# Clearing the last sums behind the last value product, leftover mixer groups behind the last projections, late weight loads deferred

## The chip, the cores and the metric

The kernel runs on one core of a Trainium2 chip. Its time is the device time of one launch in microseconds (us); where several runs are made, their median stands for the kernel. A core has five engines with queues of their own: TensorE (PE, matrix products; its weight loads are shown as PEld), VectorE (DVE), ScalarE (ACT), GpSimd (POOL) and SyncE (SP), which here only issues transfers (DMA) between HBM and the on-chip memory SBUF. Matrix products write to PSUM, an accumulator memory of eight banks per partition; a bank holds 512 columns in f32.

## The reference

Two layers are computed one after the other with the same weights. Each is an attention block and then a mixer over the tokens, both with a residual sum (S = 2048 tokens, D = 640, 32 heads of 20, F = 1536):

```python
def _A_ref(x, wqkv, wo):
    qkv = (x @ wqkv).reshape(B, S, 3, H, Dh).transpose(2, 0, 3, 1, 4)
    q, k, v = qkv[0], qkv[1], qkv[2]
    scores = jnp.einsum("bhqd,bhkd->bhqk", q, k) * (Dh ** -0.5)
    p = _softmax(scores, axis=-1)
    o = jnp.einsum("bhqk,bhkd->bhqd", p, v)
    return o.transpose(0, 2, 1, 3).reshape(B, S, D) @ wo

def _B_ref(x, w1, b1, w2, b2):
    h = _layernorm(x, axis=-1)
    u = _gelu(jnp.einsum("bsd,sf->bdf", h, w1) + b1)
    y = jnp.einsum("bdf,fs->bds", u, w2) + b2
    return y.transpose(0, 2, 1)

x = A_x
x = x + _A_ref(_layernorm(x, axis=-1), A_wqkv, A_wo)
x = x + _B_ref(_layernorm(x, axis=-1), B_w1, B_b1, B_w2, B_b2)
x = x + _A_ref(_layernorm(x, axis=-1), A_wqkv, A_wo)
x = x + _B_ref(_layernorm(x, axis=-1), B_w1, B_b1, B_w2, B_b2)
```

The weights and x are bf16; sums and the residual are kept in f32.

## The kernel before

**Tiling.** The 2048 tokens are 16 tiles of 128 and 4 blocks of 512. The 32 heads are 8 groups of 4; a group's heads lie in the four quarters of 32 partitions, so that four products of 32 rows run side by side. A unit of attention is one group, one block of queries and one tile of keys: four products of 128 keys by 512 queries, called cells. Cells are collected into tiles of three and two PSUM banks in turn (`S`, pools `s3` and `s2`), and ACT turns each tile into exponentials with one instruction (L710). Some cells go to the bank `Dt` instead, and DVE and POOL compute their exponentials with shifts and polynomials (L539 to L599). The products with the values (L1252, `emit_PV`) sum in the bank `acc`. At the end of a block DVE transposes, divides by the sum of exponentials and transposes back (`finish_run`, L747 to L771); the result is `attnT`.

**Planner.** `attention` writes the order of PE, DVE, ACT and POOL by hand: while the program is built it keeps a clock for each engine (`pem["t"]`, `dvm["t"]`, `acm["t"]`) from fixed costs, and puts whatever fits into the gaps beside the exponentials. These fillers (`add_fill`, `fill_step`) are projections of keys, queries and values, transposes, output projections, and the mixer's first product. Each filler group sums in a bank (`misc` or `Dt`), and its evacuation is a `Proc` of rank 1 that `submit` hands to the clocks of DVE or ACT. Outside of attention `submit` puts the evacuation into the program at once (`force`). Where a gap stays empty, products with zero weights (`zero_wave`, L699) keep PE busy. `landing[tt]` is the time at which the planner expects tile tt of x.

**The start of layer 0** (`TokenFeed.begin`, from L1425). SP loads x tiles 0 to 3, the first halves of the key and query weights (`w_raw`, through `load_raw` and `load_w`, L1431) and of the value weights (into `x1last`), then x tiles 4 and 5, the second halves of the three weights, and then x tiles 6 to 15 (L1439), each as soon as the tile six places ahead is normalized: its buffer is one of six. DVE takes the statistics (L823, L826), POOL the root (L840), DVE normalizes (L844), PE transposes (L1151), and the fillers for values (L1127), keys and queries (L1103) follow. ACT copies the first four groups of key and query weights into their padded form (L1474), DVE the second four (L1476).

**The end of an attention.** The mixer's first product is summed over the tokens in parts. The last part but one (L994, 6 matmuls of 128 x 320 per group, two groups per row tile of F) is among the fillers, and each group is added to a row held in SBUF (L1002). What is left of them when the last exponential has been issued is emitted behind the last value products, with banks from `tail_alloc`: `Dt`, `misc` and the third bank of `sums[0]` in turn. Then `end_tiles` handles the last two token tiles: it clears the two `S` tiles (`sums`) with four zero waves of 512 columns, ACT copies the residual into them (L893) and loads the table for GELU (L894), PE adds the projection of the last pair of head groups (L898), and DVE, ACT and POOL normalize twice over (L908 to L926): statistics of each tile, ACT's copy back to SBUF (L909), ACT's normalized first tile (L923), DVE's second (L926). Meanwhile PE runs `WARM_WAVES` = 14 zero waves of four matmuls.

**The mixer.** `mixer_head` multiplies the last two tiles with w1 (L1665), adds the row (L1668), takes GELU (L1671) and starts the second product with w2 (L1687; whole tiles in L1678). In layer 0 it feeds the start of layer 1 (`MixFeed`); in layer 1 it runs through all 16 tiles and writes the output (L1737, L1742). The weights w2 are loaded in eight parts of 768 KB (L1700), the residual in tiles of 320 KB (`x1in`, L1553 and L1718). `after_vector(inst)` makes an instruction wait for the last DVE instruction that is already in the program.

Of the kernel before, what the change touches and what calls it, by code (L numbers as in the profile page):

```python
# [23 lines left out]
D = 640  # L24
# [22 lines left out]
HALF = 0.14  # L47
# [19 lines left out]
WARM_WAVES = 14  # L67
# [10 lines left out]
def kernel(  # L78
# [12 lines left out]
    nc = tc.nc  # L91
# [128 lines left out]
    def attention(st, x_in_ap, x_mid, uacc_l, feed, feed_stack):  # L220
# [65 lines left out]
        class Proc:  # L286
# [17 lines left out]
            def step(self):  # L304
# [8 lines left out]
                if not self.steps:  # L313
                    self.eng["procs"].remove(self)
                    if self.after is not None:
                        self.after(end)

        def submit(proc):
            proc.eng["procs"].append(proc)
            if not in_attention[0]:  # L320
                force(proc)
# [562 lines left out]

        def end_tiles(sums):
            assert check_hT_dead() and TAIL == 2
            gp = NG // 2 - 1
            attnT = attnT_tiles[LASTQB + 1][gp]
            for t in sums:
                for c in (0, 512):  # L890
                    zero_wave(t[:, c:c + 512], True, True)
            for t, x1 in zip(sums, x1_end):
                nc.scalar.copy(out=t[:, 0:D], in_=x1)  # L893
            nc.scalar.activation(out=warm_act[:, 0:1], in_=mhalf[:, 0:1], func=ACT.Gelu_apprx_tanh, scale=1.0)  # L894
            for ttl, t in enumerate(sums):
                for odd in range(2):
                    for c0, c1 in Y_CUTS:
                        pe(nc.tensor.matmul(t[:, c0:c1], lhsT=attnT[:, 256 * odd + ttl * 128:256 * odd + (ttl + 1) * 128],  # L898
                                            rhs=wo_pad[:, 2 * gp + odd, c0:c1], start=False, stop=(odd == 1),
                                            skip_group_check=True))  # L900
            halves = [[t[:, 0:D // 2], t[:, D // 2:D]] for t in sums]
            st = [stat.tile([128, 2, nc.vector.BN_STATS_DIM], F32, name="bnst") for _ in range(2)]
# [8 lines left out]
            def spread(i):  # L911
# [12 lines left out]
                                 scale=rs[0][:, 0:1])  # L924
            spread(1)
            nc.vector.tensor_scalar(out=h2_view[:, NT - 1, :], in0=x1_end[1], scalar1=mv[1][:, 0:1], scalar2=rs[1][:, 0:1],  # L926
                                    op0=ALU.subtract, op1=ALU.mult)

        def add_fill(key, prio, mms, evac, w, ready=0.0, allow=None, after=None, wave=None, cells=None, cost=None,
# [446 lines left out]
        sums = [s_tile(w)[:].rearrange("p a b -> p (a b)") for w in (3, 2)]  # L1376
        tail_banks = deque([Dbank.alloc, misc.alloc, lambda: sums[0][:, 1024:1536]])

        def tail_alloc():
            tail_banks.rotate(-1)  # L1380
            return tail_banks[-1]()
        while fs["cur"] is not None or fill_queue:
            fill_step(tail_alloc)
        assert not dvm["procs"] and not acm["procs"]
        end_tiles(sums)
        idle = pp["acc"].tile([128, 512], F32, name="acc")
        for _ in range(WARM_WAVES):
            zero_wave(idle, True, True)
        p1.close()

    class TokenFeed:
# [33 lines left out]
        def begin(self, cx):  # L1425
# [4 lines left out]
            def load_w(dst, coff):  # L1430
                nc.sync.dma_start(out=dst, in_=A_wqkv[:, coff:coff + D // 2].rearrange("(dt p) n -> p dt n", p=128))  # L1431

# [12 lines left out]
            for tt in range(4, 6):  # L1445
                load_x(tt)
            load_raw(0, 1)
            load_raw(1, 1)
            load_w(self.wv[:, 1], 2 * D + D // 2)
            landing = {tt: 3.2 + 0.5 * tt for tt in range(4)}  # L1450
# [38 lines left out]
            def start_tile(tt):  # L1489
# [5 lines left out]
                def after(e):  # L1495
                    if tt + 6 < NT:
                        load_x(tt + 6)
                        landing[tt + 6] = max(14.0 + 0.5 * (tt - 2), e + 3.0)
                        start_tile(tt + 6)
                    cx.t_fill(tt, h[tt], e + DVE_TO_PE, lambda: out_h.discard(tt))  # L1500
                cx.ln_proc(xin[tt][:], False, dst, 2.5 + 0.01 * tt, landing[tt], after,
# [293 lines left out]
```

## Time and profile before

| | us |
|---|---|
| median of 3 runs | 1771.04 (1770.96 to 1772.27) |
| the profiled execution | 1772.69 |
| its span | 1770.9 |
| PE busy | 1683.8 (95%) |
| ACT busy | 1676.4 (95%) |
| DVE busy | 1538.4 (87%) |
| POOL busy | 386.6 (22%) |
| first and last exponential of layer 0 | 17.72 and 825.52 |
| first and last exponential of layer 1 | 866.50 and 1699.73 |

The granted clock of TensorE is 0.999 of full speed over the execution. The profile shows one execution; its time is that of the launch, and its span is from the first to the last instruction on the core. Lines such as L710 are lines of the kernel before. A matmul's shown end is modelled, and successive instructions of one engine overlap by a part of a microsecond, so that the time from one start to the next is shorter than the shown length. "Idle before" is the time in which an engine stood still ahead of an instruction, with what ended it.

### The profile page before, as it was taken

To read this page: it belongs to the slowest core of one execution; us is meant where nothing else is said; L and a number is where in the kernel's file an instruction comes from. 1 tells how busy PE (TensorE), PEld (TensorE's weight loads), DVE (VectorE), ACT (ScalarE), POOL (GpSimd) and SP (SyncE) were. 2 spreads that over 40 slices of the span, in tenths; PEclk is the share of its full clock that TensorE was granted. 3 is DMA by queue.
4 is the path that set the end of the run, shared out by engine and by line. 5 is a ranking of instruction groups with operands and counts; after the bars stand their busy time and mean duration, and the time that the engine had idled before them with its cause. 6 is when DMAs were issued, how large, how long until landed. Compare 5 with 4: busy or idle time off the path is not lost. (4 is left out here: it accounts for less than half of the span.)

```text
span 1770.9 us, 42935 instructions
## 1 busy us (share of the span) xinstructions
PE 1683.8 (95%) x17978; PEld 671.5 (38%) x18058; DVE 1538.4 (87%) x2361; ACT 1676.4 (95%) x1509; POOL 386.6 (22%) x599
## 2 busy tenths in 40 slices
PE   8999999999999999999999999999999999999999
PEld 3333333333333344444444433233333333444445
DVE  7479999999999999998543369999999999999972
ACT  8999999999999999998779999999999999999970
POOL 2112222232233223221000011122223232322200
PEclk9999999999999999999999999999999999999999
DMA  3200000010112110123322110000001220101345
GB/s 116 37 4 1 1 2 2 12 35 2 35 52 81 38 36 14 39 75 118 111 81 73 40 35 1 1 2 31 31 1 61 68 80 13 61 3 54 103 120 178
DMA packets 103010, 81.85 MB, mean 46 GB/s; under 512 B 50976, under 2 KB 87456, under 8 KB 102816
## 3 DMA queue, kind: packets, MB, share of 16 engines
q1 hardware_dynamic: 97280, 71.22, 13.4%
q0 software_dynamic: 5536, 7.88, 1.4%
q8 instruction: 141, 2.31, 0.6%
q14 instruction: 53, 0.43, 0.1%
HBM read 55.48 MB, written 23.59 MB: 45 GB/s over the span
## 5 line engine op out<-in xcount | busy, mean ns | idle before, releaser
L710 ACT ACTIVATE P<-S 128x1536 bf16<-128x1536 f32 (+2 forms) x1441 | 1629.0, 1368 | 15.6 <-PE S L640 15.3
L640 PE MATMUL S<-QTq,KT 32*128 32x512 bf16 (+1 forms) x4484 | 580.2, 337 | 68.9 <-ACT P L710 49.6
L599 POOL TENSOR_SCALAR ey<-ew 128x512 f16<-128x512 uint16 x496 | 306.7, 618 | 1017.2 <-DVE et L573 387.3
L640 PEld LDWEIGHTS <-KT 32*128 32x128 bf16 x5134 | 234.3, 91 | 537.9 <-issue 509.4
L1252 PE MATMUL acc<-P,Vaug 128*32 128x512 bf16 (+1 forms) x4470 | 361.5, 344 | 0.8 <-ACT P L710 0.3
L539 DVE TENSOR_SCALAR ew<-Dt 128x512 int32<-128x512 f32 x498 | 339.4, 681 | 18.7 <-PE Dt L640 12.4
L699 PE MATMUL acc<-zr,zw 128*32 128x512 bf16 x4436 | 344.0, 383 | 1.4 <-POOL zr L151 1.2
L582 DVE SCALAR_TENSOR_TENSOR Pd<-ew,et 128x1024 int16<-128x1024 int16 x249 | 310.7, 1248 | 1.5
L573 DVE SCALAR_TENSOR_TENSOR et<-ey,ew 128x1024 f32<-128x1024 f16 x249 | 303.5, 1219 | 2.0
L640 PE MATMUL Dt<-QTq,KT 32*128 32x512 bf16 (+1 forms) x650 | 191.5, 332 | 0.0
L569 DVE TENSOR_TENSOR ey<-ey 128x1024 f16<-128x1024 f16 x249 | 172.6, 693 | 0.5
L1252 PEld LDWEIGHTS <-Vaug 128*32 128x32 bf16 x5120 | 101.5, 94 | 169.1 <-issue 159.4
L699 PEld LDWEIGHTS <-zw 128*32 128x32 bf16 x4636 | 116.2, 96 | 100.6 <-issue 53.7
L840 POOL TENSOR_TENSOR rstd<-veps,mhalf 128x1 f32<-128x1 f32 x60 | 54.3, 906 | 252.8 <-DVE veps L838 206.5
L1252 PE MATMUL acc<-Pd,Vaug 128*32 128x512 bf16 (+1 forms) x650 | 97.5, 334 | 0.7 <-issue 0.5
L1103 PE MATMUL misc<-hh,wq_pad 128*128 128x512 bf16 x277 | 82.6, 383 | 2.1 <-issue 1.6
L994 PEld LDWEIGHTS <-w1st 128*128 128x128 bf16 x672 | 52.6, 97 | 57.6 <-issue 44.7
L747 DVE STREAM_TRANSPOSE T<-acc 128x512 f32<-128x512 f32 (+1 forms) x81 | 56.3, 695 | 20.4 <-PE acc L1252 20.0
L1043 PE MATMUL misc<-wo_pad,attnT 128*128 128x320 bf16 x384 | 73.5, 302 | 0.3 <-DVE x1s L1055 0.2
L994 PE MATMUL misc<-x1last,w1st 128*128 128x320 bf16 x384 | 71.6, 302 | 0.0
L1103 PE MATMUL misc<-hh,wk_pad 128*128 128x512 bf16 x211 | 64.8, 383 | 2.0 <-issue 1.3
L359 DVE CAST KT<-misc 128x512 bf16<-128x512 f32 x48 | 32.8, 683 | 19.8 <-PE misc L1103 19.7
(145 smaller groups left out, 1085.9 us busy)
## 6 DMA issues: line engine op xcount, KB each, us to landing
w2s<-in_B_w_dram SPq DMA_DIRECT2D x16, 768.0 KB
uacc<-ustg POOLq DMA_DIRECT2D x24, 320.0 KB, 2.7
x1in<-xd SPq DMA_DIRECT2D x24, 320.0 KB
w1st<-in_B_w_dram SPq DMA_DIRECT2D x24, 256.0 KB
xd<-x2s SPq DMA_DIRECT2D x16, 320.0 KB
xin<-xd SPq DMA_DIRECT2D x16, 320.0 KB
w1st<-in_B_w_dram SPq DMA_DIRECT2D x24, 192.0 KB
xd<-x1s SPq DMA_DIRECT2D x12, 320.0 KB
```

The lines of the kernel that those rows point to most:

```text
L539: nc.vector.tensor_scalar(out=w[:, slot, :], in0=Dt[:, :], scalar1=127.0 * FIX, scalar2=0.0, op0=ALU.add, op1=ALU.max)
L569: nc.vector.tensor_tensor(out=y, in0=y, in1=y, op=ALU.mult)
L573: nc.vector.scalar_tensor_tensor(out=box["t"][:, 0:512 * k], in0=ve_y.pop(p)[:, 0:512 * k], scalar=MANT_C * MANT_K ** 2, in1=frac, op0=ALU ...
L582: nc.vector.scalar_tensor_tensor(out=bits, in0=whole, scalar=128.0, in1=box["t"][:, 0:512 * k], op0=ALU.mult, op1=ALU.add)
L599: return engine.tensor_scalar(out=out_ap, in0=in_ap, scalar1=MANT_K / FIX, scalar2=-MANT_K * MANT_S, op0=ALU.mult, op1=ALU.add)
L640: pe(nc.tensor.matmul(out_ap[:, c0:c0 + w], lhsT=KT[32 * j:32 * j + 32, g, kt * 128:(kt + 1) * 128], rhs=get_QT(st, qb)[32 * j:32 * j + 32 ...
L699: pe(nc.tensor.matmul(bank[32 * j:32 * j + 32, 0:w], lhsT=zw[:], rhs=zr[:, :, 0:64].to_broadcast([128, w // 64, 64]), start=start, stop=st ...
L710: nc.scalar.activation(out=P[:, 0:ncs, :].rearrange("p a b -> p (a b)"), in_=St[:, 0:ncs, :].rearrange("p a b -> p (a b)"), func=ACT.Exp, ...
L994: pe(nc.tensor.matmul(t[:, 0:w], lhsT=w1_of[(p, ft)][:, sti, :], rhs=rows_in[sti][:, c0:c1], start=(sti == 0), stop=(sti == n_in - 1)))
L1043: pe(nc.tensor.matmul(t[:, 0:w], lhsT=attnT[g][:, ttl * 128:(ttl + 1) * 128], rhs=wo_pad[:, g, c0:c1], start=(g == 0), stop=(g == NG - 1)))
L1103: pe(nc.tensor.matmul(t[:, :], lhsT=wpad[:, dt_, g, :], rhs=hT[:, dt_, tb * 512:(tb + 1) * 512], start=(dt_ == 0), stop=(dt_ == NDT - 1)))
L1252: pe(nc.tensor.matmul(acc[32 * j:32 * j + 32, a0:a0 + w], lhsT=Vaug[:, (kt * H + hh_) * VW:(kt * H + hh_) * VW + 32], rhs=P[:, slot, c0:c0 ...
```

## The change

It has three parts.

In `TokenFeed.begin` the second halves of the key, query and value weights are no longer loaded behind x tiles 4 and 5. `load_rest` issues them when tile 5 has been normalized, and each of these loads waits for the DVE instruction that is then the last one in the program (`after_vector`). The planner's expected landing of x tile tt + 6 becomes 16.5 + 0.5 tt instead of 14.0 + 0.5 (tt - 2).

Behind the last value product the two sums are cleared at once, each with a wave of 512 columns and one of 128 instead of two of 512. Then leftover fillers are emitted for 1.3 us of the planner's clock, and a group that is begun is finished.

In `end_tiles`, fillers that are then still left come behind the last projections. Their evacuations are held (`held`) and put into the program later: one while POOL computes the second root, the others behind the last normalized tile. The number of warming waves falls by four for each such group, and not below four.

```diff
--- before.py
+++ after.py
@@ -315,8 +315,13 @@
                     if self.after is not None:
                         self.after(end)
 
+        held = []
+
         def submit(proc):
             proc.eng["procs"].append(proc)
+            if not in_attention[0] and proc.rank == 1 and held:
+                held.append(proc)
+                return
             if not in_attention[0]:
                 force(proc)
 
@@ -882,13 +887,12 @@
             ln_open.append(tt)
             ln_proc(x1s[:], True, dst, 3, end + DVE_NEXT, after)
 
-        def end_tiles(sums):
+        rest_fills = [0]
+
+        def end_tiles(sums, alloc):
             assert check_hT_dead() and TAIL == 2
             gp = NG // 2 - 1
             attnT = attnT_tiles[LASTQB + 1][gp]
-            for t in sums:
-                for c in (0, 512):
-                    zero_wave(t[:, c:c + 512], True, True)
             for t, x1 in zip(sums, x1_end):
                 nc.scalar.copy(out=t[:, 0:D], in_=x1)
             nc.scalar.activation(out=warm_act[:, 0:1], in_=mhalf[:, 0:1], func=ACT.Gelu_apprx_tanh, scale=1.0)
@@ -898,6 +902,16 @@
                         pe(nc.tensor.matmul(t[:, c0:c1], lhsT=attnT[:, 256 * odd + ttl * 128:256 * odd + (ttl + 1) * 128],
                                             rhs=wo_pad[:, 2 * gp + odd, c0:c1], start=False, stop=(odd == 1),
                                             skip_group_check=True))
+            held.append(None)
+            while fs["cur"] is not None or fill_queue:
+                fill_step(alloc)
+            rest_fills[0] = len(held) - 1
+            held.pop(0)
+
+            def emptied(n):
+                while n and held:
+                    force(held.pop(0))
+                    n -= 1
             halves = [[t[:, 0:D // 2], t[:, D // 2:D]] for t in sums]
             st = [stat.tile([128, 2, nc.vector.BN_STATS_DIM], F32, name="bnst") for _ in range(2)]
             mv = [stat.tile([128, nc.vector.BN_AGGR_DIM], F32, name="mv") for _ in range(2)]
@@ -923,8 +937,10 @@
             nc.scalar.activation(out=h2_view[:, NT - 2, :], in_=x1_end[0], func=ACT.Identity, bias=shift[:, 0:1],
                                  scale=rs[0][:, 0:1])
             spread(1)
+            emptied(1)
             nc.vector.tensor_scalar(out=h2_view[:, NT - 1, :], in0=x1_end[1], scalar1=mv[1][:, 0:1], scalar2=rs[1][:, 0:1],
                                     op0=ALU.subtract, op1=ALU.mult)
+            emptied(len(held))
 
         def add_fill(key, prio, mms, evac, w, ready=0.0, allow=None, after=None, wave=None, cells=None, cost=None,
                      act=None, gate=None, fed=False):
@@ -1374,17 +1390,21 @@
             emit_PV(n)
 
         sums = [s_tile(w)[:].rearrange("p a b -> p (a b)") for w in (3, 2)]
-        tail_banks = deque([Dbank.alloc, misc.alloc, lambda: sums[0][:, 1024:1536]])
+        for t in sums:
+            zero_wave(t[:, 0:512], True, True)
+            zero_wave(t[:, 512:D], True, True, HALF / 2, D - 512)
+        tail_banks = [sums[0][:, 1024:1536], None, None]
 
         def tail_alloc():
-            tail_banks.rotate(-1)
-            return tail_banks[-1]()
-        while fs["cur"] is not None or fill_queue:
+            bank = tail_banks.pop()
+            return bank if bank is not None else Dbank.alloc() if len(tail_banks) == 1 else misc.alloc()
+        room = pem["t"] + 1.3
+        while fs["cur"] is not None or (fill_queue and pem["t"] < room):
             fill_step(tail_alloc)
+        end_tiles(sums, tail_alloc)
         assert not dvm["procs"] and not acm["procs"]
-        end_tiles(sums)
         idle = pp["acc"].tile([128, 512], F32, name="acc")
-        for _ in range(WARM_WAVES):
+        for _ in range(max(4, WARM_WAVES - 4 * rest_fills[0])):
             zero_wave(idle, True, True)
         p1.close()
 
@@ -1428,7 +1448,9 @@
             raw, xin = {}, {}
 
             def load_w(dst, coff):
-                nc.sync.dma_start(out=dst, in_=A_wqkv[:, coff:coff + D // 2].rearrange("(dt p) n -> p dt n", p=128))
+                inst = nc.sync.dma_start(out=dst, in_=A_wqkv[:, coff:coff + D // 2].rearrange("(dt p) n -> p dt n", p=128))
+                if (0, 1) in raw:
+                    after_vector(inst)
 
             def load_raw(i, part):
                 raw[(i, part)] = self.wp.tile([128, NDT, D // 2], BF16, name="w_raw")
@@ -1444,9 +1466,11 @@
             load_w(self.wv[:, 0], 2 * D)
             for tt in range(4, 6):
                 load_x(tt)
-            load_raw(0, 1)
-            load_raw(1, 1)
-            load_w(self.wv[:, 1], 2 * D + D // 2)
+
+            def load_rest():
+                load_raw(0, 1)
+                load_raw(1, 1)
+                load_w(self.wv[:, 1], 2 * D + D // 2)
             landing = {tt: 3.2 + 0.5 * tt for tt in range(4)}
             landing.update({4: 9.5, 5: 10.0})
             wpads = (wk_pad, wq_pad)
@@ -1495,8 +1519,10 @@
                 def after(e):
                     if tt + 6 < NT:
                         load_x(tt + 6)
-                        landing[tt + 6] = max(14.0 + 0.5 * (tt - 2), e + 3.0)
+                        landing[tt + 6] = max(16.5 + 0.5 * tt, e + 3.0)
                         start_tile(tt + 6)
+                    if tt == 5:
+                        load_rest()
                     cx.t_fill(tt, h[tt], e + DVE_TO_PE, lambda: out_h.discard(tt))
                 cx.ln_proc(xin[tt][:], False, dst, 2.5 + 0.01 * tt, landing[tt], after,
                            allow_apply=lambda: len(out_h) < 4, cheap=0.04)
```

## The prediction

> **What bounds the kernel now.** I read the stretches of both attentions first, then ScalarE's (ACT's) timeline, then the start and the two ends of attention in order of time, and last the chain that ended last.
>
> In the timeline of ACT alone (start, length, line, kind, count, in brackets the idle time before and what ended it), layer 0's exponentials are two unbroken rows:
>
> ```profile
> 17.72 495.66 ACT L710 ACTIVATE P<-S 128x1536 bf16<-128x1536 f32 x438 [3.14 <-PE S L640]
> 513.53 311.99 ACT L710 ACTIVATE P<-S 128x1536 bf16<-128x1536 f32 x276 [0.16 <-PE acc L1252]
> ```
>
> From 17.72 to 825.52 ACT stands still for 0.16 us, so layer 0 lasts as long as its 714 exponentials. Only three things count there: when the first one starts, how many there are, and what follows the last.
>
> The groups of ACT by shape, in the window of 17 to 826 us, give the mix:
>
> ```profile
> L710 ACT ACTIVATE P<-S 128x1536 bf16<-128x1536 f32 x357 | 564.6, 1582 | 3.5 <-PE S L640 3.1 <-PE acc L1252 0.2
> L710 ACT ACTIVATE P<-S 128x1024 bf16<-128x1024 f32 x356 | 413.9, 1163 | 0.0
> ```
>
> Neighbours overlap, so the means are no steps. The means differ by 0.42 us for 512 columns. Together with one tile of 512, 714 tiles in 807.6 us give a step s of a 1024 tile: 714 s + 357 x 0.42 - 0.42 = 807.6, so s = 0.92 us.
>
> The timeline of the start shows why the first exponential is at 17.72:
>
> ```profile
> 9.19 28.23 SPq L1439 DMA_DIRECT2D x0in<-in_A_x_dram  x10
> 14.12 0.68 DVE L359 CAST KT<-Dt 128x512 bf16<-128x512 f32 x1
> 14.85 0.84 PE L1127 MATMUL Dt<-x1last,hh 128*128 128x320 bf16 x5 [0.46 <-DVE KT L359]
> 16.15 0.49 DVE L823 BATCH_NORM_STATS2 bnst<-x0in 128x6 f32<-128x320 bf16 x1 [1.35 <-DMA x0in<-in_A_x_dram]
> 16.56 0.67 DVE L361 TENSOR_SCALAR QTq<-misc 128x512 bf16<-128x512 f32 x1
> 17.29 0.59 PE L640 MATMUL S<-QTq,KT 32*128 32x512 bf16 x5 [1.59 <-DVE QTq L361]
> ```
>
> VectorE (DVE) waits 1.35 us for tile 6 of x, whose load SP issues at 9.19, behind the three late weight loads. The copy of the first Q stands behind those statistics, and scores and exponentials behind it.
>
> The timeline of layer 0's end:
>
> ```profile
> 825.96 0.85 PE L994 MATMUL misc<-hh,w1st 128*128 128x320 bf16 x5
> 827.18 0.45 DVE L771 STREAM_TRANSPOSE attnT<-T 128x256 bf16<-128x256 bf16 x1
> 828.87 0.98 PE L994 MATMUL S<-hh,w1st 128*128 128x320 bf16 x6
> 830.43 1.05 PE L699 MATMUL S<-zr,zw 128*32 128x512 bf16 x16 [0.58 <-DVE KT L1002]
> 831.13 1.32 ACT L893 COPY S<-x1last 128x640 f32<-128x640 f32 x2 [5.61 <-PE S L699]
> 831.88 1.33 PE L898 MATMUL S<-wo_pad,attnT 128*128 128x512 bf16 x7 [0.41 <-ACT S L893]
> 832.47 1.28 ACT L894 ACT_TABLE_LOAD   x1
> 833.76 0.20 ACT L894 ACTIVATE warm_act<-mhalf 128x1 f32<-128x1 f32 x1
> 836.51 1.25 PE L1665 MATMUL um<-hh,KT 128*128 128x512 bf16 x7 [0.17 <-ACT hh L923]
> ```
>
> The last attention rows are there at 827.63, but the last projections begin 4.25 us later: 23 leftover mixer matmuls, then the evacuation of one that used the sum's bank, then the clearing and ACT's copy stand between. The same place in layer 1, with 12 leftover matmuls and attnT ready at 1701.78:
>
> ```profile
> 1700.12 0.99 PE L994 MATMUL Dt<-hh,w1st 128*128 128x320 bf16 x6
> 1701.86 1.05 PE L699 MATMUL S<-zr,zw 128*32 128x512 bf16 x16
> 1702.57 1.32 ACT L893 COPY S<-x1last 128x640 f32<-128x640 f32 x2 [2.84 <-issue]
> 1703.31 1.33 PE L898 MATMUL S<-wo_pad,attnT 128*128 128x512 bf16 x7 [0.41 <-ACT S L893]
> ```
>
> From there the chain of waits is matmuls almost without a break (L1665, L1687, L1678) up to 1763.65, so time won ahead of it reaches the end.
>
> **Part 1, the deferred loads.** In the changed program as built, SP issues x tiles 4 to 11 ahead of the late weights. DVE's order is the old one up to the key copy at 14.12; then come the Q copy and a value copy, and only then the statistics of tile 6. A neighbour follows a 0.68 us copy after 0.60 us (19.26 to 19.85), so the Q copy runs from 14.72 to 15.40. TensorE (PE) has the value group of 14.85 ahead of the scores: five matmuls at 0.14 us to 15.55, which binds. Scores to exponential took 0.43 us (17.29 to 17.72), so the first exponential comes at 15.98: 1.7 us gained. Tile 6 cannot spoil it: its load follows tile 0's apply (5.81 + 0.43), some 2.8 us sooner than 9.19 and without 1.23 MB ahead of it, and it is wanted after 16.1 us.
> What is late next? SP reaches the weights after tile 5's apply (13.76 + 0.45 = 14.2) and x tile 11; three issues of 0.55 to 1.06 us end near 16.5. Tile 6 of before landed 7 us after its issue behind such a load; taken as the upper bound, the weights are there at 23.5. DVE's weight copies (L1476) began at 28.35, so now near 26.6: 3 us of cover. Behind SP's new wait stand x tiles 12 to 15, whose statistics began at 38.19. Bounds of this part: 0 to -1.74; I take -1.7, since every row on the path is shown.
>
> **The rewritten plan.** The planner now expects tile 6 at 16.5 us instead of 13.0 (it was there at 16.15), so all of layer 0 is ordered anew. As built, DVE takes 496 score tiles instead of 498, and ACT one more 128x1024 tile. With ACT without a gap that is +0.92 us. Layer 1's order is the old one up to its end, so it only shifts. New gaps in ACT's train are not shown; from the 0.16 us of before I put them at 0, up to +1.
>
> **Part 2, the end of layer 0.** As built, 16 clearing matmuls stand straight behind the last value product (8 of them 128 wide), then 6 leftover matmuls, then the projections. On the old clock: clearing from 825.96, two wide waves at 0.22 and two narrow at 0.06 (the step of the 128-wide L1687) to 826.52; six L994 at 0.14 to 827.35. ACT's copies, 0.66 each, follow the first cleared sum near 826.5 and end at 827.82; the second is wanted 0.55 us after the projections begin. So attnT (827.63), with a weight load of 0.10, decides: projections at 827.78 instead of 831.88, -4.1 us. The one leftover evacuation (0.47) fits on DVE between 827.63 and the statistics at 828.6 (0.81 behind the projections, as 831.88 to 832.69). From projections to the mixer's first matmul the 4.63 us stay, as DVE's four statistics and the second copy set them. Bounds: the loads of w2 and x1in, which waited for the last L994 and were done by 838, move 2.5 us or so, not 4.1; w2's first use was at 839.40. That leaves -3.4 to -4.3.
>
> **Part 2, the end of layer 1.** Clearing 1700.12 to 1700.68, twelve L994 to 1702.34, copies by 1701.98: the projections come at 1702.4 instead of 1703.31, -0.9. PE is the last one here, so bounds are -0.5 to -1.1. The w2 loads wait for the last L994, now 0.45 us later, and are wanted at 1710.83: covered.
>
> **Part 3, the held groups.** As built, no leftover group stands behind the last projections in either layer, and the 56 warming matmuls stay. This part does nothing here: 0 us. If it worked, it could save at most the 1.66 us of layer 1's twelve matmuls less the 1.1 us in which attnT is awaited.
>
> **The table load.** The row at 832.47 lasts 1.28 us and ACT goes on at 833.76, without a pause. The Trainium skill (ScalarE: Activation LUTs, "What ACT_TABLE_LOAD costs") adds a drain of about 1.38 us to each load, 2.66 in all. The trace shows none here. By that rule the sum would be about 0.4 us worse.
>
> **Sum.** -1.7 + 0.9 - 4.1 - 0.9 = -5.8 us. The profiled execution took 1772.69 with a span of 1770.9, so it would become 1766.9. The median of the three runs, 1771.04, is 1.65 below that execution; it becomes 1765.2.
>
> **Rivals.**
> Start lost: the first exponential is earlier, but ACT then waits for the second key group, whose matmuls keep their place. For it: DVE was busy 7.85 of 8 us in 16 to 24. Against: that group's Q copy ended 4.2 us after the first exponential, and the first group feeds ACT for 7.2 us (16 cells of 512 columns; ACT's train holds 357 x 3 + 356 x 2 + 1 = 1784 of them in 807.6 us). Then -4.1: 1766.9.
> Loads decide layer 0's end: the mixer head waits for w2 or x1in, half of the 4.1 is lost: 1767.3. Against: 2.2 MB took 8 us up to 838, and x1in was first used at 848.58.
> Table load: if ACT is held 1.28 us longer behind it, the two copies back to SBUF are late in layer 0 alone (832.78 instead of 832.38 on the old clock for the mixer's first matmul): 1765.6.
> Small gaps: the new order leaves ACT waiting 1 to 3 us in sum: 1767.5.
> Slower: in the new order a key block of a later x block comes late and ACT waits once as it did in layer 1 from 888.34 to 896.67, 8.34 us, for scores behind DVE's copies: 1773.5. It turns the sign once such gaps exceed 5.8 us. For it: all of layer 0 is ordered anew. Against: x now lands earlier than the plan expects, and with x 3 us later than planned ACT had no gap.
>
> **Numbers.** Forecast 0.62, start lost 0.14, loads 0.09, table 0.03, small gaps 0.06, slower 0.06. No change means within 0.2%, 1767.5 to 1774.6, about what a measurement of this kernel can tell. Faster takes the forecast, the table, three quarters of the first rival, half of the second and of the small gaps: 0.83; slower, beyond 1774.6, takes half of the last, where more than one such wait comes: 0.03; the rest, 0.14, is the same. Range: the best bounds give -1.74 + 0.92 - 4.3 - 1.1 = -6.2, the runs' own spread 1 us more: 1764.0; upward it takes in the first three rivals: 1768.0.
>
> **What would show it.** First exponential near 16.0; 715 exponentials and no gap over 0.5 us up to about 824.7; projections 1.75 us behind the start of the clearing in layer 0, 2.3 in layer 1; the late weights landed before L1476. An ACT gap of microseconds in layer 0, or DVE waiting for w_raw, would make it wrong.

## The result, and the profile after

Six runs of the changed kernel have a median of 1764.70 us (1764.62 to 1766.10); six of the kernel before, taken beside them, 1771.03 (1770.54 to 1772.27). The ratio is 0.9965, with an interval of 0.9952 to 0.9978: 6.3 us faster. The profiled execution of the changed kernel took 1764.66, with a span of 1762.8 and a granted clock of 1.000. Lines have moved: L710 is now L715, L994 is L1010, L699 is L704, L893 is L897, L898 is L902, L1002 is L1018, L1665 is L1691.

Five distances, read from the two timelines, hold the whole difference of the spans, 8.1 us:

| us | before | after | |
|---|---|---|---|
| first exponential of layer 0 | 17.72 | 16.01 | -1.71 |
| layer 0's exponentials, first start to last end | 807.80 | 808.20 | +0.40 |
| last exponential of layer 0 to the mixer's first matmul | 10.99 | 6.41 | -4.58 |
| from there to layer 1's first exponential | 29.99 | 30.00 | 0 |
| layer 1's exponentials | 833.23 | 832.04 | -1.19 |
| last exponential of layer 1 to the mixer's first matmul | 8.21 | 7.21 | -1.00 |
| from there to the end | 62.98 | 62.97 | 0 |

The medians differ by 6.3, not 8.1: the row of layer 1's exponentials belongs to the profiled execution of before, and a part of the first row too, as the experiments show.

Layer 0's exponentials in ACT's timeline of the changed kernel (start, length, line, kind, count, idle time before and what ended it):

```profile
16.01 486.21 ACT L715 ACTIVATE P<-S 128x1536 bf16<-128x1536 f32 x430 [1.49 <-PE S L645]
502.38 321.83 ACT L715 ACTIVATE P<-S 128x1536 bf16<-128x1536 f32 x285 [0.16 <-PE acc L1268]
```

They are 715, again with one idle time of 0.16 us: no new gap. The timeline of the start, all engines:

```profile
14.06 0.68 DVE L364 CAST KT<-Dt 128x512 bf16<-128x512 f32 x1
14.55 1.00 SPq L1451 DMA_DIRECT2D w_raw<-in_A_wqkv_dram  x2
14.66 0.68 DVE L366 TENSOR_SCALAR QTq<-misc 128x512 bf16<-128x512 f32 x1
15.57 0.60 PE L645 MATMUL S<-QTq,KT 32*128 32x512 bf16 x5
16.16 0.48 DVE L828 BATCH_NORM_STATS2 bnst<-x0in 128x6 f32<-128x320 bf16 x1
```

The query copy stands right behind the key copy. The statistics of tile 6 come at 16.16, as late as in the kernel before (16.15), but nothing on the path stands behind them. The late weights are issued at 14.55. The end of layer 0:

```profile
824.47 0.70 PE L704 MATMUL S<-zr,zw 128*32 128x512 bf16 x13
824.98 1.32 ACT L897 COPY S<-x1last 128x640 f32<-128x640 f32 x2 [0.78 <-PE S L704]
825.11 0.99 PE L1010 MATMUL misc<-hh,w1st 128*128 128x320 bf16 x6
825.75 0.45 DVE L776 STREAM_TRANSPOSE attnT<-T 128x256 bf16<-128x256 bf16 x1
825.80 0.23 PEld L902 LDWEIGHTS <-attnT 128*128 128x128 bf16 x2
825.93 1.31 PE L902 MATMUL S<-wo_pad,attnT 128*128 128x512 bf16 x8
826.25 0.66 PEld L902 LDWEIGHTS <-attnT 128*128 128x128 bf16 x6 [0.22 <-DVE attnT L776]
826.32 1.28 ACT L898 ACT_TABLE_LOAD   x1
826.80 0.90 DVE L922 BATCH_NORM_STATS2 bnst<-S 128x6 f32<-128x320 f32 x2 [0.18 <-PE S L902]
827.62 0.20 ACT L898 ACTIVATE warm_act<-mhalf 128x1 f32<-128x1 f32 x1
```

Clearing, copies and six leftover matmuls lie beside DVE's work on the last rows. Two weight loads of attnT (825.80) do not wait for the last transposition, which ends at 826.20; the other six do (826.25). And the end of layer 1:

```profile
1692.93 0.74 PE L704 MATMUL S<-zr,zw 128*32 128x512 bf16 x16
1693.60 0.99 PE L1010 MATMUL misc<-hh,w1st 128*128 128x320 bf16 x6
1694.26 0.45 DVE L776 STREAM_TRANSPOSE attnT<-T 128x256 bf16<-128x256 bf16 x1
1694.42 0.98 PE L1010 MATMUL Dt<-hh,w1st 128*128 128x320 bf16 x6
1695.24 1.25 PE L902 MATMUL S<-wo_pad,attnT 128*128 128x512 bf16 x8
```

Here PE works without a break from the clearing to the projections, 0.53 us past the end of the transposition (1694.71).

### The profile page after: what moved, and what is told of

Its sections match the earlier page's. It is cut to its first block, busy times and chain, and to the rows that moved or that the text cites. A ratio compares the mean times of both kernels' runs of the same rounds, so it can differ in the third digit from the quotient of the medians.

```text
span 1762.8 us, 42985 instructions
## 1 busy us (share of the span) xinstructions
PE 1686.9 (96%) x18044; PEld 669.7 (38%) x18044; DVE 1536.8 (87%) x2356; ACT 1676.8 (95%) x1510; POOL 379.6 (22%) x597
## 5 line engine op out<-in xcount | busy, mean ns | idle before, releaser
L715 ACT ACTIVATE P<-S 128x1024 bf16<-128x1024 f32 (+1 forms) x1442 | 1629.2, 1387 | 13.0 <-PE S L645 12.7
L704 PE MATMUL acc<-zr,zw 128*32 128x512 bf16 x4408 | 343.8, 383 | 1.2 <-POOL zr L151 1.2
L704 PEld LDWEIGHTS <-zw 128*32 128x32 bf16 x4620 | 116.9, 96 | 99.5 <-issue 54.7
L845 POOL TENSOR_TENSOR rstd<-veps,mhalf 128x1 f32<-128x1 f32 x60 | 49.0, 817 | 252.3 <-DVE veps L843 197.3
L1119 PE MATMUL misc<-hh,wq_pad 128*128 128x512 bf16 x300 | 87.3, 383 | 0.0
L1010 PEld LDWEIGHTS <-w1st 128*128 128x128 bf16 x672 | 52.1, 97 | 58.6 <-issue 46.5
L1119 PE MATMUL misc<-hh,wk_pad 128*128 128x512 bf16 x250 | 73.2, 383 | 0.0
L1010 PE MATMUL misc<-x1last,w1st 128*128 128x320 bf16 x384 | 72.1, 302 | 0.0
```

The costliest lines, as they stand in the source:

```text
L704: pe(nc.tensor.matmul(bank[32 * j:32 * j + 32, 0:w], lhsT=zw[:], rhs=zr[:, :, 0:64].to_broadcast([128, w // 64, 64]), start=start, stop=st ...
L715: nc.scalar.activation(out=P[:, 0:ncs, :].rearrange("p a b -> p (a b)"), in_=St[:, 0:ncs, :].rearrange("p a b -> p (a b)"), func=ACT.Exp, ...
L1010: pe(nc.tensor.matmul(t[:, 0:w], lhsT=w1_of[(p, ft)][:, sti, :], rhs=rows_in[sti][:, c0:c1], start=(sti == 0), stop=(sti == n_in - 1)))
L1119: pe(nc.tensor.matmul(t[:, :], lhsT=wpad[:, dt_, g, :], rhs=hT[:, dt_, tb * 512:(tb + 1) * 512], start=(dt_ == 0), stop=(dt_ == NDT - 1)))
```

## The experiments

The distances of all kernels, each read from the timelines of its profiled execution. "Start" is the first exponential; "to P" and "to M" run from a layer's last exponential to its last projections and to the mixer's first matmul.

| kernel | median us | start | layer 0 to P | to M | layer 1 to P | to M |
|---|---|---|---|---|---|---|
| before | 1771.03 | 17.72 | 6.36 | 10.99 | 3.58 | 8.21 |
| before_again | 1770.82 | 17.83 | 6.35 | 10.98 | 3.59 | 8.22 |
| defer_only | 1770.06 | 16.29 | 6.35 | 10.99 | 3.58 | 8.21 |
| landing_only | 1766.60 | 15.95 | 2.73 | 7.36 | 3.58 | 8.21 |
| start_only | 1766.79 | 16.07 | 2.73 | 7.37 | 3.59 | 8.22 |
| tail_only | 1770.49 | 17.09 | 3.35 | 10.72 | 2.58 | 7.21 |
| tail_misc | 1767.00 | 17.03 | 3.34 | 7.97 | 2.58 | 7.21 |
| tail_ahead | 1770.83 | 17.83 | 6.49 | 11.12 | 2.57 | 7.20 |
| no_defer | 1764.61 | 15.96 | 1.72 | 6.41 | 2.58 | 7.22 |
| after | 1764.70 | 16.01 | 1.72 | 6.41 | 2.58 | 7.21 |
| wide | 1765.38 | 16.35 | 2.05 | 6.68 | 2.90 | 7.53 |
| room08 | 1763.84 | 15.97 | 1.74 | 6.44 | 1.76 | 6.48 |
| land45 | 1764.58 | 15.30 | 1.73 | 6.42 | 2.58 | 7.21 |
| room08_land45 | 1764.09 | 15.38 | 1.73 | 6.42 | 1.77 | 6.48 |

### Is the excess of the first profile its own?

before_again is the kernel before, unchanged.

> The kernel before, unchanged, for a second profiled execution of it. The first one read 1772.69, 1.65 above its own median. Theory A (the excess was that one execution's: some 1.2 in the second layer's exponentials, the rest in the first layer's): time 1771.0, span near 1769.2, the second layer's exponentials 832.0 from first to last instead of 833.23, the first layer's near 807.3 instead of 807.80. Theory B (the excess is how the old order always runs): 833.2 and 807.8 again, span 1770.9.

Median 1770.82 (10 runs, 1770.30 to 1774.07); but the execution that was profiled this time is the slowest of them, 1774.07. Layer 1's exponentials took 833.22 once more, and a gap is new at the start of layer 0. ACT's timeline there:

```profile
17.83 2.37 ACT L710 ACTIVATE P<-S 128x1536 bf16<-128x1536 f32 x2 [3.34 <-PE S L640]
21.34 2.37 ACT L710 ACTIVATE P<-S 128x1536 bf16<-128x1536 f32 x2 [1.15 <-PE S L640]
```

The clock in this trace is at 0.5 from 17.72 to 21.13, over the first two exponentials and the matmuls that the third waits for. Taken by itself this profile speaks for theory B. The other kernels settle it: defer_only and landing_only have the old tails, and their layer 1 took 832.03 and 832.04; start_only, with the same tails, took 833.23. Windows over the same stretch of layer 1 (us; PE's busy time and instructions; granted clock; DMA) show what differs. The kernel before, from the end of its 8.34 us gap on:

```profile
896.67:902.44 5.77, 4.91 (x40) 0.82 0.54 189
902.44:906.60 4.16, 4.11 (x28) 0.84 0.00 0
```

The changed kernel in the same place:

```profile
890.79:896.50 5.71, 4.66 (x45) 1.00 0.51 181
896.50:899.52 3.02, 3.02 (x21) 1.00 0.00 0
```

The clock in the trace of before is at 0.5 from 900.35 to 903.77. The same work lasts 9.93 us there and 8.73 here: 1.2 us, which is the 1.19 of the table. The ten runs of before_again show both in one kernel: the six with a granted clock of 1.000 over their span take 1770.30 to 1770.85, the four with 0.998 or 0.999 take 1771.69 to 1774.07. So it comes and goes with the execution, and theory A holds for it. The earlier start does not go the same way: five profiles with the old order and the old place of the loads have their first exponential at 17.72, 17.83, 17.09, 17.03 and 17.83. The first profile was a late one among these, not an exception. In all five DVE's first statistics of tile 6 wait for its load, until 15.46 to 16.26, so the start varied with that landing.

### Which of the start's two edits brings what?

The start's change has two edits, the deferred loads and the landing number. They were tried with the old tails, alone (defer_only, landing_only) and together (start_only), and the full change was run without the deferral (no_defer). The landing number alone:

```diff
-                        landing[tt + 6] = max(14.0 + 0.5 * (tt - 2), e + 3.0)
+                        landing[tt + 6] = max(16.5 + 0.5 * tt, e + 3.0)
```

> The old tails with the deferred weight loads and the new landing number. The plan then holds 6 leftover groups at the end of the first layer instead of 23. Theory A (the reordered clearing and the shorter list of leftovers share the first layer's end): first exponential 16.0 (-1.7), exponential train +0.4 to +0.9, first layer's end about -3 of the -4.6 because only 6 leftovers stand ahead of the clearing, second layer's end unchanged: 1767.3. Theory B (the first layer's end comes from the clearing's place alone): end of the first layer unchanged, 1769.8 to 1770.2.

> The changed kernel with its late weight loads issued at the old place, ahead of the last x tiles; landing number and tails as changed. Theory A as put in the prediction (deferral brings x tile 6 earlier and that gives the start): first exponential 17.4 to 17.7, time 1766.1 to 1766.4. Theory B (the landing number alone moves tile 6's statistics behind the Q copy on VectorE, its arrival doesn't matter): first exponential 16.0, time 1764.7 within 0.2.

> Old tails and old landing number, only the late weight loads deferred. The plan is the old one: on VectorE tile 6's statistics still stand ahead of the first query copy, 23 leftovers at the first layer's end. Theory A (deferral works, but only where the order puts the statistics first: tile 6 lands earlier, the 1.35 us of waiting ahead of the statistics goes): first exponential 16.2 to 16.5 instead of 17.1 to 17.8, everything behind it as before, 1769.3 to 1769.9. Theory B (tile 6 does not land earlier than about 16.1 for another reason): first exponential 17.1 to 17.8, 1770.7.

> Old tails, late weight loads at their old place, only the planned landing of x changed. Theory A (the number alone rewrites the order of the first layer and brings both the early first exponential and the short list of leftovers): first exponential 16.0, 6 leftovers at the first layer's end, projections 2.7 behind the last exponential, time as with both, 1766.6 within 0.3. Theory B (with the loads at the old place tile 6 or later tiles come late and ScalarE waits among its first exponentials): a gap there of 0.5 us or more, 1767.1 or above.

no_defer takes 1764.61 (5 runs, 1764.57 to 1764.62), the changed kernel's time, and theory B holds: with the loads at the old place the first exponential comes at 15.96. landing_only and start_only agree in the same way, 1766.60 (theory A) and 1766.79. So the number in the planner brings the whole start, and the deferral adds nothing to it. defer_only shows that the deferral does work by itself, in DVE's timeline:

```profile
14.13 0.68 DVE L359 CAST KT<-Dt 128x512 bf16<-128x512 f32 x1
14.73 0.48 DVE L823 BATCH_NORM_STATS2 bnst<-x0in 128x6 f32<-128x320 bf16 x1
15.13 0.67 DVE L361 TENSOR_SCALAR QTq<-misc 128x512 bf16<-128x512 f32 x1
```

The statistics still stand ahead of the query copy, but tile 6 is there, and the 1.35 us of waiting are gone: first exponential at 16.29, as theory A has it, and 1770.06 (11 runs, 1769.96 to 1771.29) against 1770.71, 0.16 above the range of that theory. Two ways out of one wait: bring the data earlier, or let nothing urgent stand behind it. Either is enough, and the second gains 0.3 us more, because the statistics' own 0.40 us go behind the query copy too.

landing_only brings a larger thing that has nothing to do with the start: its plan leaves 6 matmuls at the end of layer 0 instead of 23, and the old tail, unchanged, reaches the mixer 3.63 us sooner. The end of layer 0 in start_only:

```profile
824.63 0.99 PE L994 MATMUL Dt<-hh,w1st 128*128 128x320 bf16 x6
825.54 1.05 PE L699 MATMUL S<-zr,zw 128*32 128x512 bf16 x16
826.25 1.32 ACT L893 COPY S<-x1last 128x640 f32<-128x640 f32 x2 [1.99 <-PE S L699]
827.00 1.33 PE L898 MATMUL S<-wo_pad,attnT 128*128 128x512 bf16 x7 [0.41 <-ACT S L893]
```

Leftovers, clearing, copies and projections still follow each other. Clearing first (the changed kernel) takes a further 0.96 us out of layer 0 and 1.0 out of layer 1, and the medians say the same: 1766.60 less 1764.61 is 1.99. Theory A of start_only holds, with 3.6 us at layer 0's end where it put about 3, and 1766.79 for its 1767.3.

### What does the tail do when 23 matmuls are left?

tail_only has the old start, and so 23 leftovers, of which 12 are held behind the projections: part 3 at work, which it never is in the changed kernel.

> The old start with the new tails. The plan leaves 23 groups at the first layer's end, of which 11 stand ahead of the projections and 12 are held behind them. Theory A (a held group costs nothing, the projections wait for the 11 and the clearing): first exponential 17.7, first layer's projections about 2.5 behind the last exponential instead of 6.4 (-3.8), second layer's end -1.0: 1766.2. Theory B (the held groups and the copies out of their PSUM tiles delay the mixer's first matmul or the next stage): first layer's end -2.5 or less, 1767.5 to 1768. If the first layer's end needs no shorter list at all: -4.6 and 1765.4.

Median 1770.49 (11 runs: ten from 1769.52 to 1773.86, with a median of 1770.43, and one of 4276.25 that stands alone); theory B, and worse than it: the projections come 3.0 us sooner, the mixer's first matmul 0.27. The timeline of layer 0's end tells why:

```profile
828.25 1.25 PE L902 MATMUL S<-wo_pad,attnT 128*128 128x512 bf16 x7
830.15 0.98 PE L1010 MATMUL S<-hh,w1st 128*128 128x320 bf16 x6
831.24 0.90 DVE L922 BATCH_NORM_STATS2 bnst<-S 128x6 f32<-128x320 f32 x2 [2.30 <-PE S L1010]
835.62 2.65 PE L1685 MATMUL um<-hh,KT 128*128 128x512 bf16 x10 [3.08 <-DVE KT L1018]
```

The last held group sums in the third bank of the tile whose first two banks hold the first sum. DVE's statistics of that sum wait for the tile, and so for matmuls that they have no use for: 2.30 us. They come 2.99 us behind the projections, where tail_misc below has 0.81, and PE, its 24 warming matmuls done at 832.5, stands still. That wait ends with DVE's evacuation of the same bank (KT, L1018, 834.99 to 835.47), not with ACT's normalized tile as in tail_misc. In all the mixer's first matmul is 7.37 us behind the projections instead of 4.63. The windows (PE busy and granted clock are the second and fourth numbers):

```profile
832.60:835.60 3.00, 0.00 (x0) 1.00 0.99 294
835.60:838.50 2.90, 2.66 (x11) 0.54 0.60 196
```

The mixer begins at half the clock; from its first matmul to layer 1's first exponential it takes 30.88 instead of 30.0. tail_misc puts that one group into another bank:

```diff
-        tail_banks = [sums[0][:, 1024:1536], None, None]
+        tail_banks = [misc.alloc, Dbank.alloc, misc.alloc]
...
-            return bank if bank is not None else Dbank.alloc() if len(tail_banks) == 1 else misc.alloc()
+            return tail_banks.pop()()
```

> Old start, new tails, but the last held group of the first layer sums in misc instead of the third bank of the first sum's tile. With that third bank the statistics of the first token tile waited 2.30 us for the held group's matmuls, the mixer's first matmul came 7.37 us behind the projections instead of 4.69, TensorE stood still for 3.08 us, and the granted clock fell to 0.5 for 3.4 us. Theory A (the shared tile causes the wait, the rest follows from it): statistics 0.8 behind the projections, mixer's first matmul near 5.0 behind them, no clock window at 0.5 there, from the mixer's first matmul to the next exponential 30.0 instead of 30.88; time 1767.2. Theory B (the held evacuations on VectorE and the 24 instead of 56 warming matmuls cause it): 7 us and 30.9 again, 1770.5.

1767.00 (11 runs, 1766.44 to 1768.68): theory A. Its timeline in the same place:

```profile
829.00 0.90 DVE L922 BATCH_NORM_STATS2 bnst<-S 128x6 f32<-128x320 f32 x2
830.09 0.98 PE L1010 MATMUL misc<-hh,w1st 128*128 128x320 bf16 x6
832.82 1.25 PE L1684 MATMUL um<-hh,KT 128*128 128x512 bf16 x8 [0.35 <-ACT hh L937]
```

The statistics run ahead of the held group's matmuls, PE waits 0.35 us, and the next exponential follows 30.00 behind. The 24 warming matmuls and the two evacuations on DVE cost next to nothing: 4.63 us from the projections to the mixer. One bank was worth 3.5 us.

tail_ahead holds nothing and leaves all 23 matmuls ahead of the projections:

```diff
-        room = pem["t"] + 1.3
+        room = pem["t"] + 9.0
```

> Old start, new clearing, but all leftover groups stay ahead of the last projections (23 matmuls in the first layer): nothing is held. Theory A (clearing straight behind the last value product is worth about 1 us in each layer, by the 0.96 and 1.0 that the full change gains over the one without it): first layer's projections 5.2 to 5.5 behind the last exponential instead of 6.36, mixer's first matmul 9.8 to 10.1 instead of 10.99, second layer -1.0; time 1768.6. Theory B (ahead of so many leftovers the clearing is hidden in the first layer anyway, a bank that the leftovers wait for decides): first layer unchanged, second -1.0; 1769.6.

1770.83 (11 runs, 1769.72 to 1773.32): theory B for layer 0, where the clearing gains nothing (6.49 against 6.36), while layer 1 gains its 1.0. The median hides that gain: the five lowest runs take 1769.72 to 1769.97, near theory B's 1769.6, and the other six, the profiled one with its start at 17.83 among them, 1770.83 and more. The same shared tile is in the way, now of ACT's copies into it:

```profile
829.81 0.98 PE L1010 MATMUL S<-hh,w1st 128*128 128x320 bf16 x6
831.39 1.32 ACT L897 COPY S<-x1last 128x640 f32<-128x640 f32 x2 [5.75 <-issue]
832.14 1.33 PE L902 MATMUL S<-wo_pad,attnT 128*128 128x512 bf16 x8 [1.35 <-ACT S L897]
```

The copies start 0.08 us behind DVE's evacuation of the third bank (830.82 to 831.31, L1018); the releaser is not named in the row, so that they wait for it is read from the order of the rows. PE has its first weight load of attnT at 830.49 and then waits 1.35 us for the copies. Together: with 23 leftovers the tail as changed is worth 0.27 us in layer 0, with its third bank moved 3.0, with all leftovers ahead nothing; with 6 leftovers it is worth 0.96.

### Who is last ahead of the projections?

wide clears with two waves of 512 columns again, at the new place.

```diff
-            zero_wave(t[:, 512:D], True, True, HALF / 2, D - 512)
+            zero_wave(t[:, 512:1024], True, True)
```

> The changed kernel with the second clearing wave of each sum 512 instead of 128 columns wide, at the same place. Two waves become longer by 0.22 less 0.06, 0.32 us in all, in each layer. Theory A (TensorE is the last one ahead of the projections in the second layer, and in the first layer within 0.1 us of the last transposition): second layer's projections 2.9 instead of 2.58 behind the last exponential, the first layer's 2.04 instead of 1.72 for the first product and 0.1 to 0.3 later at the mixer's first matmul; 1765.2 within 0.2. Theory B (ACT's copies or the transposition of attnT decide in both layers): no change, 1764.7.

1765.38 (6 runs, 1765.17 to 1766.41). Layer 1's projections come 0.32 us later, as many as PE has more to do, layer 0's 0.33 and its mixer 0.27. Theory A: PE is last in layer 1; in layer 0 it and the transposition of attnT are within 0.06 us of each other, since the mixer moves by 0.27 of the 0.33. (0.34 us more in this profile is its start at 16.35.)

### Is part 3 worth anything?

room08 is the changed kernel with `room = pem["t"] + 0.8` instead of 1.3. It holds one group, in layer 1, in the bank `Dt`.

> The changed kernel with 0.8 instead of 1.3 us of leftover groups ahead of the last projections: in the second layer one group of six matmuls (bank Dt) comes behind them, its evacuation is held, and 40 warming matmuls run instead of 56. The first layer is as changed. Theory A (a held group outside the sums' own tile is nearly free): the second layer's projections come 0.5 us earlier (2.1 behind the last exponential instead of 2.58), the mixer's first matmul 0.3 to 0.5 earlier; 1764.3. Theory B (a held group always costs, through its evacuation on VectorE or because TensorE stands idle and loses its clock): the mixer's first matmul 0.5 to 1.5 later; 1765.2 to 1766.2.

1763.84 (5 runs, 1763.79 to 1764.24; against before 0.9960, interval 0.9948 to 0.9973), 0.86 below the changed kernel and below all its runs. Theory A, with a larger size than it put (1764.3): the mixer comes 0.73 earlier and the start 0.04; the last 0.09 of the medians is in no row. Layer 1's end in its timeline:

```profile
1694.22 0.45 DVE L776 STREAM_TRANSPOSE attnT<-T 128x256 bf16<-128x256 bf16 x1
1694.25 0.23 PEld L902 LDWEIGHTS <-attnT 128*128 128x128 bf16 x2
1694.38 1.33 PE L902 MATMUL S<-wo_pad,attnT 128*128 128x512 bf16 x8
1694.72 0.66 PEld L902 LDWEIGHTS <-attnT 128*128 128x128 bf16 x6 [0.24 <-DVE attnT L776]
1695.55 0.98 PE L1010 MATMUL Dt<-hh,w1st 128*128 128x320 bf16 x6
1699.10 1.25 PE L1691 MATMUL um<-hh,KT 128*128 128x512 bf16 x8 [0.30 <-ACT hh L937]
```

The first two projections run while DVE still transposes, as they do in layer 0, and the six held matmuls run beside DVE's statistics. Layer 1's end now has the distances of layer 0's.

### Earlier still at the start

land45 gives x tiles 4 and 5 planned landings of 13.5 and 14.0 instead of 9.5 and 10.0, so that more of DVE's work falls behind the first key copy; room08_land45 has both edits.

> The changed kernel with the planned landing of x tiles 4 and 5 at 13.5 and 14.0 instead of 9.5 and 10.0. As built, the normalization of these tiles falls behind the first key copy on VectorE. Theory A (what counts is what stands ahead of the first key and query copies on VectorE, not when tiles land): first exponential near 15.5 instead of 16.0, 0.3 to 0.5 gained, 1764.3. Theory B (the values and scores of the later tiles come late in turn, ScalarE waits among the first exponentials): first exponential earlier, a gap of 0.5 to 2 us behind it, 1764.7 to 1766.

> Both: 0.8 us of leftovers ahead of the last projections, and the planned landings 13.5 and 14.0 for x tiles 4 and 5. Alone the first gave 1763.84; the second brought the first exponential from 16.01 to 15.30, but in its profiled execution TensorE waited 0.59 us for a part of w2 between the layers and the next layer's exponentials began 0.65 later. Theory A (that wait is systematic: the weight's load sets the start of the next layer): first exponential 15.3, from the mixer's first matmul to the next exponential 30.5 to 30.7, 1763.7. Theory B (it was that one execution's): 30.0 there, 1763.1 to 1763.3.

The first exponential does come earlier, at 15.30 and 15.38, and no gap follows. But land45's median is 1764.58 (5 runs, 1764.56 to 1766.43), 0.12 below the changed kernel, so its theory A has the start and not the time. The two together, 1764.09 (1764.01 to 1764.23), are 0.25 slower than room08 alone. In land45's profile PE waits between the layers:

```profile
852.44 1.80 PE L1623 MATMUL Dt<-uT,w2s 128*128 128x320 bf16 x12 [0.59 <-DMA w2s<-in_B_w_dram]
```

In room08_land45 it does not (29.99 from the mixer's first matmul to the next exponential, theory B), yet the time is not theory B's 1763.1 to 1763.3, so that wait does not explain the loss. There layer 0's exponentials take 808.36 instead of 808.20, and layer 1's 832.53 instead of 832.04, with the same gaps and the same 727 tiles. The last row of layer 1's exponentials holds the difference, first in room08, then in room08_land45:

```profile
907.91 784.71 ACT L715 ACTIVATE P<-S 128x1024 bf16<-128x1024 f32 x694 [1.06 <-PE S L645]
907.48 785.20 ACT L715 ACTIVATE P<-S 128x1024 bf16<-128x1024 f32 x694 [1.05 <-PE S L645]
```

By the single starts that this row merges, two steps make it up: from the 576th tile to the 577th takes 1.16 us instead of 0.90, and from the 704th to the 705th 1.40 instead of 1.11; the other differences nearly cancel. land45 has the same two steps, and its layer 1 agrees: 833.72 less the 1.19 us of a clock at 0.5, which its trace shows from 894.87 to 898.28, is 832.53. So most of what is won at the start is paid back in the exponentials; why these two steps are longer stays open. By the spans of the two profiled executions, 1762.08 and 1762.14, room08_land45 is only 0.06 behind room08; the rest of the 0.25 is in no row.

## Why the prediction was right, and where its steps were not

**The first exponential.** Time and order were as put: 15.98 forecast, 16.01 measured, with TensorE's value group and not the query copy setting it. The heading was wrong: it is not the deferred loads (no_defer, 15.96). The sum took 17.72 as the start of before; other executions start at 17.0 to 17.8, so against the median this term is nearer to -1.0 than to -1.7. That is worked out from another kernel: defer_only, which starts only 0.28 later than the changed kernel, has a median 0.65 below that of before.

**One more exponential.** Forecast +0.92, measured +0.40. The tile does take a step: its start-to-start time in the trace is 0.90. But some steps are longer, by up to 0.5 us, which the merged rows do not show: what goes beyond the usual 1.331 us (for 1536 columns) and 0.904 (for 1024) adds up to 10.1 us in layer 0 of before and 9.4 in that of the changed kernel. The rewritten order has 0.7 less of it, while its last exponential is shown 0.2 longer (0.86 and 0.66). The prediction put new gaps between 0 and +1 and left out that they could be fewer.

**The end of layer 0.** Forecast -4.1, measured -4.58 (the mixer's first matmul). The failed step is "attnT, with a weight load, decides": two of the eight projections read the half of attnT that was finished before, so only six are behind the transposition, and that was done 2.00 us behind the last exponential, not 2.11. The statistics of the first sum came 2.59 us behind the last exponential, against 3.07 as put (827.78 and 0.81, less 825.52). What the term hid is that it is two gains: 3.63 from the rewritten plan, which left 6 matmuls instead of 23, and 0.96 from the order of clearing and leftovers. The evacuation fitted in front of the statistics (826.13), and the loads of w2 and x1in were not late, as put.

**The end of layer 1.** Forecast -0.9 with PE last; measured -1.0, and wide confirms who is last.

**The held groups.** Nothing, as put, in the changed kernel. The bound on what they could save (1.66 less 1.1, 0.56) was too small: room08 saves 0.73 at the mixer and 0.86 by the medians, because again two projections need not wait for attnT. And the prediction gave part 3 no bound on the side of loss; by tail_only it gives back 2.7 us of the projections' 3.0, and 0.9 more behind the mixer's start.

**The late weights.** The copies of them on DVE (L1500) began at 28.94 without a wait, not near 26.6, and 0.6 later than before. From the bound of 23.5 that is 5.4 us of cover, not 3; when the weights landed the trace does not show.

**The table load.** The load at 826.32 lasts 1.28 us and ACT's next instruction starts at 827.62, as in before. The Trainium skill (ScalarE: Activation LUTs, "What ACT_TABLE_LOAD costs") has a drain of about 1.38 us on top; neither trace shows it, and the rival that hung on it is out. So are the others: the second key group kept ACT fed, no x block came late, no load held the mixer.

**The median.** Subtracting the profile's 1.65 us of excess from the forecast was right in sum. 1.19 us of it are the lowered clock in layer 1; that the rest is the start's lateness is inferred, as no execution of before near its median was profiled. Against the median the terms are about -1.0, +0.4, -4.6 and -1.0, together -6.2 for the measured 6.3; the forecast's -5.8 had 0.7 too much in the first, and 1.1 too little in the others (0.5 in the extra exponential, 0.5 and 0.1 in the two ends). So the sum is nearer than its terms, and that is luck: the errors have opposite signs.

## What to carry to other kernels

Where a planner writes the order, ask for each edit of its numbers what is left over at the end of the plan: here a landing time at the start was worth 3.6 us at the end of the layer, more than the reordering made for that place. A leftover that is put behind the critical step is free only if it writes no tile that the critical step reads or waits for; one shared tile turned a gain of 3 us into 0.3. When a step waits for "the" result of another engine, look which part of it each instruction reads: halves that are finished earlier move the start.

## What was unexpected of the hardware

The granted clock of TensorE falls to 0.5 for one stretch of 3.41 us, or not, in executions of one kernel: at 900.35 and 901.77 in two profiles of before, at 895.50 in start_only, at 894.87 in land45, at 17.72 in before_again, at 835.84 in tail_only; in the nine other profiles not before the last matmuls. Each time in layer 1 cost 1.2 us. The Trainium skill (TensorE: Matmul & The Clock Gate, "Part 1: The HAM clock gate") has free-running windows of about 3.4 us and half the clock after at least one idle window. The length agrees, and tail_only comes near: PE stood still for 3.08 us, from 832.54 to 835.62, and in the 3.41 us ahead of the fall at 835.84 it was busy for 0.33. The stretches at 900 do not agree: in the 3.41 us ahead of one PE was busy for 2.55. The changed kernel has the same 2.55 at the same distance behind layer 1's first exponential, and its clock stays at 1.000. The lines of the windows, of before and of the changed kernel:

```profile
896.94:900.35 3.41, 2.55 (x26) 1.00 0.82 293
891.06:894.47 3.41, 2.55 (x26) 1.00 0.76 276
```

Those are transpositions and scores with waits of 0.2 to 0.5 us between them. That the same work passes in other executions would fit a window that lies differently over it, but no run here moved the window, so this stays a reading.
